# A fused long-convolution and gated-MLP kernel: first rows in four transfers, the norm's power by row tile on GpSimd, a new order of work, last waits in order of the stores

## The chip, the cores and the metric

One NeuronCore of a Trainium2 chip runs the whole program in one launch. The metric is device time in microseconds (us), from the start of an execution to its end. Engines are named as in the profile: PE (TensorE; PEld is its weight load), DVE (VectorE), ACT (ScalarE), POOL (GpSimd) and SP (SyncE, which here only issues DMAs; ACT issues some too).

## The reference

All tensors are bfloat16; x = A_q is 2048 x 512, the filter ssm_k is 512 x 2048, the MLP weights are 512 x 1792, 512 x 1792 and 1792 x 512.

```python
xn = (x - mean(x)) / sqrt(var(x) + 1e-5)             # over the 512 features
# A: H3 branch
k_shift[s] = sum over t<4 of k[s - 3 + t] * shift_k[:, 3 - t]
kv = k_shift * v
y = causal_convolution(kv, ssm_k)                    # by FFT of length 4096 over 2048 positions
s = xn * (y + kv * ssm_D)
# B: gated MLP on the same xn
g = silu((gelu_tanh(xn @ w_gate) * (xn @ w_up)) @ w_down)
out = x + s * g
```

## The kernel before, in words

**Layout.** Partition p holds rows 16p to 16p+15 of x, k, v and the output, so "row tile t" (t = 0 to 15) is row 16p+t of every partition. Row tiles are worked in four groups q of four.

**The norm, `ln(q)`, line 805.** For each row tile `bn_stats` (L808) and `bn_aggr` (L809) on DVE put mean and variance into `mv`. For q = 0 the four tiles go in two halves of two, for q > 0 all four at once: DVE adds the epsilon (L816), POOL raises to the power -0.5 (L817), and DVE normalises each tile (`XN`, L820). For q = 0 and 1 PE transposes each XN tile (L841) into `xnT`; for q = 2 and 3 a DMA transpose does.

**The filter and the convolution.** The filter arrives in four pieces h0 to h3 of 128 channels (`Hn`). PE transposes them (L865), ACT or DVE copies the result to `HTr`, and PE multiplies it by the first stage F1 of a two-stage transform (`stage1`, line 900). The results go to DRAM scratch `ZH` by DMAs that ACT issues and come back rearranged as `BH` for the second stage. The product kv takes the same road: `kshift(i)`, line 939, makes k_shift * v for the four row tiles of group i on DVE (a product into `KAC`, L956; three products into `KTM`, L960, each added to KAC, L962; the product with `V`, L964). It needs the loads k0 to k(i), v(i) and the taps. `stage1("K", u)` multiplies V by F1 on PE, ACT or DVE copies it to `AST` or `ASX`, and SP stores it to `ZK` (line 923). `spectrum(n)`, line 1028, multiplies the two spectra and goes back through `ZI`.

**The MLP.** `unit(q, m)`, line 1060: four matmuls with Wg and four with Wu, ACT's gelu (L1088) and DVE's product `HT` (L1091). `down(q)`, line 1094: 14 matmuls with Wd a row tile, then ACT and DVE (`G`, L1115 and L1117; L1123, L1125 and L1126 for the last group).

**What sets the order.** All work is declared as tasks. `SEQ` is a string of task numbers that was written by a search over the cost model in `Sched`; `Sched.run` (line 344) walks it, gives each task its engine and buffers, and the tasks are then emitted in that order. So the order in which an engine meets its instructions is the order of SEQ alone, and every engine works in order. In the model the input loads (`load`, line 580) have a queue of their own, called "loads". In the program that is emitted, they are DMAs issued by SP, in the same instruction stream as SP's stores and reads of scratch, and a wait of SP for a store's data holds up what stands behind it. SP's stream in the kernel before: x00 (row tiles 0 and 1), h0, x01 (tiles 2 and 3), h1, wg0, wu0, h3, wg1, x1, the first halo of k, wu1, h2, sk, second halo, wg3, k0, kz, wu3, wg2, wu2, D, k1, v0, k2, wd0, v1, k3, v3, v2, wd1; then the first ZK store (K0), which waits for ACT's copy to AST; then x3, the first BH, further stores, reads and transposes; at the end the 11 output stores and a wait for each. "wg1" is the second chunk of w_gate, of 512 columns.

**PE's start.** PE runs `N_WARM` matmuls on zeros (`warm_up`, line 660) before its first real work.

```python
        for t in order:
            t.emit(t.eng)
        for d in d_out:
            trk.wait_direct("SP", d.sem, d.count)
```

## Time and profile before

| what | value |
|---|---|
| median of 3 runs (lowest, highest) | 196.63 us (196.54, 197.39) |
| the profiled execution's own time | 196.41 us |
| its span, first to last instruction | 194.6 us |
| PE busy | 188.7 us (97%) |
| DVE busy | 156.7 us (81%) |
| ACT busy | 125.0 us (64%) |
| POOL busy | 11.9 us (6%) |
| DMA, mean over the span | 247 GB/s |

The span leaves 1.8 us of the profiled execution's time outside. Busy time counts instructions that compute, not waits or the issuing of DMAs. An engine's line in the profile gives start, duration, engine, line of the program, operation and tiles (out<-in).

### The profile page before, as it was taken

The numbers are of one execution on the slowest core, as the hardware profiler recorded it, in microseconds if no ns is written. First come the engines' busy times: TensorE is split into PE (matmuls) and PEld (weight loads), VectorE is DVE, ScalarE is ACT, GpSimd is POOL, SyncE is SP. The second block draws the span as 40 slices with busy tenths as digits, with TensorE's granted clock in tenths as the row PEclk, the third lists the DMA queues.
The fourth block names the chain that finished last, engine by engine and source line by source line (L and its number), as shares of the span: only waits on it lengthen the run. The fifth ranks groups of instructions, "written<-read, shape, count | busy, mean of one in ns | idle before, by whom it ended". The sixth has DMA issues, their size and how long they took to land.

```text
span 194.6 us, 3488 instructions
## 1 busy us (share of the span) xinstructions
PE 188.7 (97%) x1379; PEld 87.2 (45%) x1393; DVE 156.7 (81%) x242; ACT 125.0 (64%) x173; POOL 11.9 (6%) x26
## 2 busy tenths in 40 slices
PE   7999999999999999999999999999999999999993
PEld 2694645544444444443444343434343444444442
DVE  6898799999999997768897894788694850988984
ACT  4788897677679688876777756967674532303031
POOL 7310600000000000020200000000000000000000
PEclk9999999999999999999999999999999999999999
DMA  5999999997769967999999618986132616647363
GB/s 182 330 329 339 362 381 403 410 406 257 303 190 342 156 178 251 343 327 287 277 284 274 243 54 258 332 280 217 56 111 109 214 61 231 251 121 253 117 267 108
DMA packets 34502, 48.14 MB, mean 247 GB/s; under 512 B 8499, under 2 KB 27191, under 8 KB 34486
## 3 DMA queue, kind: packets, MB, share of 16 engines
q1 hardware_dynamic: 28982, 39.53, 63.6%
q10 hardware_dynamic: 5504, 8.39, 11.9%
q8 instruction: 11, 0.18, 0.4%
q14 instruction: 5, 0.04, 0.1%
HBM read 27.39 MB, written 14.68 MB: 216 GB/s over the span
## 4 chain that ended last, share of the span: by engine, by line
PE 93%; DVE 2%; DMA 2%; POOL 1%; issue 1%; ACT 0%
PE psall L604 86%; PE psall L979 5%; DMA X<-in_A_q_dram 2%; PE psall L865 1%; PE psall L841 1%; POOL mv L817 1%; DVE stats L808 1%; DVE G L1126 0%; DVE G L1125 0%; ACT G L1123 0%; DVE XN L820 0%; DVE mv L809 0%; DVE mv L816 0%
## 5 line engine op out<-in xcount | busy, mean ns | idle before, releaser
L604 PE MATMUL psall<-xnT,Wu 128*128 128x512 bf16 (+1 forms) x232 | 55.5, 372 | 0.0
L604 PE MATMUL psall<-xnT,Wg 128*128 128x512 bf16 (+1 forms) x232 | 55.3, 372 | 0.0
L604 PE MATMUL psall<-Wd,HT 128*128 128x512 bf16 (+2 forms) x228 | 51.0, 366 | 0.9 <-issue 0.6
L1091 DVE TENSOR_TENSOR HT<-psall,GE 128x512 bf16<-128x512 f32 x54 | 36.3, 686 | 13.1 <-PE psall L604 11.1
L1088 ACT ACTIVATE GE<-psall 128x512 bf16<-128x512 f32 x54 | 31.2, 599 | 16.5 <-PE psall L604 14.1
L604 PEld LDWEIGHTS psall<-Wd,HT 128*128 128x128 bf16 x238 | 22.1, 98 | 26.3 <-issue 1.9
L604 PEld LDWEIGHTS psall<-xnT,Wu 128*128 128x128 bf16 x232 | 21.8, 98 | 25.7 <-issue 1.8
L604 PEld LDWEIGHTS psall<-xnT,Wg 128*128 128x128 bf16 x232 | 22.1, 98 | 24.9 <-issue 1.1
L595 ACT ACTIVATE HS<-psall 128x1024 bf16<-128x1024 f32 x15 | 14.7, 1022 | 4.5 <-PE psall L979 4.5
L595 ACT ACTIVATE BO<-psall 128x1024 bf16<-128x1024 f32 x12 | 12.0, 1023 | 6.9 <-PE psall L979 6.9
L962 DVE TENSOR_TENSOR KAC<-KAC,KTM 128x2048 bf16<-128x2048 bf16 x12 | 14.6, 1219 | 0.1
L960 DVE TENSOR_TENSOR KTM<-KK,SKB 128x2048 bf16<-128x2048 bf16 x12 | 14.6, 1219 | 0.1
L595 ACT ACTIVATE KB<-psall 128x1024 bf16<-128x1024 f32 x11 | 10.9, 1023 | 5.5 <-PE psall L979 5.5
L1117 DVE SCALAR_TENSOR_TENSOR G<-G,psall 128x512 bf16<-128x512 bf16 x12 | 7.9, 683 | 6.7 <-ACT G L1115 6.7
L595 ACT ACTIVATE AST<-psall 128x1024 bf16<-128x1024 f32 x10 | 10.1, 1023 | 3.5 <-PE psall L604 3.5
L808 DVE BATCH_NORM_STATS2 stats<-X 128x6 f32<-128x512 bf16 x16 | 10.4, 681 | 0.8 <-DMA X<-in_A_q_dram 0.8
L1115 ACT ACTIVATE G<-psall 128x512 bf16<-128x512 f32 x12 | 7.0, 600 | 6.2 <-PE psall L604 6.1
L1042 DVE TENSOR_TENSOR HS<-KB,HS 128x1024 bf16<-128x1024 bf16 x16 | 10.9, 683 | 0.0
L1042 DVE TENSOR_TENSOR HW<-KB,HW 128x1024 bf16<-128x1024 bf16 x16 | 10.9, 687 | 0.0
L817 POOL TENSOR_TENSOR mv<-mv,NHALF 128x4 f32<-128x4 f32 (+1 forms) x5 | 5.7, 1148 | 83.0 <-DVE mv L816 83.0
L1123 ACT ACTIVATE G<-psall 128x512 bf16<-128x512 f32 (+2 forms) x5 | 2.6, 513 | 12.3 <-PE psall L604 12.3
L598 DVE CAST KB<-psall 128x1024 bf16<-128x1024 f32 x5 | 6.1, 1223 | 4.2 <-PE psall L979 4.2
(78 smaller groups left out, 179.3 us busy)
## 6 DMA issues: line engine op xcount, KB each, us to landing
BH<-ZH SPq DMA_DIRECT2D x8, 512.0 KB, 5.4
HW<-HS SPq DMA_DIRECT2D x16, 256.0 KB, 2.7
BK<-ZK SPq DMA_DIRECT2D x8, 512.0 KB, 5.9
ZI<-BO ACTq DMA_DIRECT2D x16, 256.0 KB, 2.6
BI<-ZI SPq DMA_DIRECT2D x8, 512.0 KB, 4.2
ZK<-AST SPq DMA_DIRECT2D x5, 512.0 KB, 3.4
Hn<-in_A_ssm_k_dram SPq DMA_DIRECT2D x4, 512.0 KB, 7.2
KK<-in_A_k_dram SPq DMA_DIRECT2D x4, 512.0 KB, 12.4
```

The lines of the kernel that those rows point to most:

```text
L595: return h.activation(o, i, ACTF.Copy, scale=scale)
L604: return h.matmul(o, lhsT=l, rhs=r, start=st, stop=sp)
L808: t_stats[t] = op([("DVE", 670.0)], lambda e, h, t=t: h.bn_stats(stats[:, t, :], X[:, t, :]), r=[bX[q][t % 4]], w=[bst[t]], rr=[R_X[t]], w ...
L817: t_pw = op([("POOL", 850.0)], lambda e, hd, ts=ts, n=n: hd.tensor_tensor(mv[:, ts, 3:4], mv[:, ts, 2:3], NHALF[:, 0:n, :], ALU.pow), r=[b ...
L960: op([("DVE", dur)], lambda e, h, j=j, m=m: h.tensor_tensor(KTM[:, m.slot, :, :], kk(j), sk(j), ALU.mult), r=need + [bSKB[j], a], w=[m], r ...
L962: op([("DVE", dur)], lambda e, h, m=m: h.tensor_tensor(KAC[:, a.slot, :, :], KAC[:, a.slot, :, :], KTM[:, m.slot, :, :], ALU.add), r=[m], ...
L979: trk.op("PE", lambda h: h.matmul(ps(s, i)[b, :], lhsT=wt(col)[a, :], rhs=data(col)[a, :], start=n < 16, stop=n >= len(todo) - 16, tile_po ...
L1042: return hd.tensor_tensor(o, flat(KB, kb[h]), o, ALU.mult)
L1088: op([("ACT", act(512))], lambda e, h: h.activation(GE[:, g.slot, :], bank(pg), ACTF.Gelu_apprx_tanh), r=[pg], w=[g], rr=lambda: R_bank(pg ...
L1091: op([("DVE", dve(512, 1))], lambda e, h: h.tensor_tensor(HT[:, q % 2, m, :], bank(pu), GE[:, g.slot, :], ALU.mult), r=[pu, g], w=[bHT[q][m]],
L1115: op([("ACT", act(n))], lambda e, h, g=g, pc=pc: h.activation(g, pc(), ACTF.Tanh, scale=0.5), r=[p], w=[bt], rr=lambda p=p: R_bank(p), ww= ...
L1117: op([("DVE", dve(512, 1))], lambda e, h, g=g, pc=pc: h.scalar_tensor_tensor(out=g, in0=g, scalar=1.0, in1=pc(), op0=ALU.add, op1=ALU.mult ...
```

## The change

- The first four row tiles are loaded in four transfers of 128 KB in place of two of 256 KB (`load_x0`). SP's stream becomes x00, x01, h0, x02, x03, wg0, wu0, h1, x1, wg1, first halo, h3, wu1, second halo, h2, sk, k0, kz, wg3, wu3, D, k1, wg2, wu2, k2, v0, wd1, wd0, v3, v1, then K0 (the first ZK store), then v2 and k3, then the first BH, x2 and so on.
- In the norm the epsilon and the power are two POOL instructions; for q = 0 they and the buffers are by row tile, and for q > 0 for four at once. DVE's addition is gone.
- The warm-up has 9 matmuls in place of 11. They read 128 columns of zeros four times over, so that the first memset is of 128 columns and the rest of it follows.
- The two products that build a table (`m_prod`, before at L701) are declared behind the four XN tiles of q = 0 (line `S.behind(t, ...)`).
- The model's landing times of the first five loads are given as numbers (`LANDS`), and SEQ is a new string: the order changes on every engine, throughout.
- The last waits of SP stand in the order in which the stores were issued.

```diff
-N_WARM = 11
-ORDER = "x00 x01 w0 w1 h0 h1 h2 h3 D0 w2 ..."
+N_WARM = 9
+ORDER = "x00 x01 h0 x02 x03 h1 w0 w1 h2 h3 D0 w2 ..."
 SEQ = (
...
+    LANDS = (3000.0, 3450.0, 5100.0, 5550.0, 6250.0)
...
+                if n_loads < len(self.LANDS):
+                    free[eng] = self.LANDS[n_loads] - self.LOAD_LAT
+                n_loads += 1
...
-        t_zero = S.add([("DVE", 250.0)], lambda e: trk.op("DVE", lambda h: h.memset(ZERO, 0.0), w=[R_zero]), w=[bwarm])
+        S.add([("DVE", 130.0)], lambda e: trk.op("DVE", lambda h: h.memset(ZERO[:, 0:128], 0.0), w=[R_zw]), w=[bzw])
+        S.add([("DVE", 200.0)], lambda e: trk.op("DVE", lambda h: h.memset(ZERO[:, 128:512], 0.0), w=[R_zero]), r=[bzw], w=[bwarm])
...
         def load_x0(t, ring):
-            load(f"x0_{t}", X[:, 2 * t:2 * t + 2, :], x_dr[:, 2 * t:2 * t + 2, :], R_X[2 * t:2 * t + 2], bX[0][2 * t:2 * t + 2], 262144, ring)
+            load(f"x0_{t}", X[:, t, :], x_dr[:, t, :], [R_X[t]], [bX[0][t]], 131072, ring)
...
-            for h in range(1 if q else 2):
-                n = 4 if q else 2
-                ts = slice(4 * q + 2 * h, 4 * q + 2 * h + n)
+            for h in range(1 if q else 4):
+                n = 1 if q == 0 else 4
+                ts = slice(4 * q + h, 4 * q + h + n)
...
-                t_var = op([("DVE", 180.0)], ... hd.tensor_scalar(mv[:, ts, 2:3], mv[:, ts, 1:2], LN_EPS, None, ALU.add) ...)
-                t_pw = op([("POOL", 850.0)], ... hd.tensor_tensor(mv[:, ts, 3:4], mv[:, ts, 2:3], NHALF[:, 0:n, :], ALU.pow) ...)
+                def pw(e, ts=ts, n=n, rm=rm):
+                    trk.op(e, lambda h: h.tensor_scalar(mv[:, ts, 2:3], mv[:, ts, 1:2], LN_EPS, None, ALU.add), r=rm, w=rm)
+                    trk.op(e, lambda h: h.tensor_tensor(mv[:, ts, 3:4], mv[:, ts, 2:3], NHALF[:, 0:n, :], ALU.pow), r=rm + [R_nh], w=rm)
+                S.add([("POOL", 430.0 + 230.0 * n)], pw, r=[bid, *bm], w=[b])
...
-        t_ln = ln(0)
+        ln(0)
         S.add([("ACT", 2400.0)], m_turn, r=[bMF], w=[bMF2])
+        for t in tm_tasks:
+            S.behind(t, [d for b in bXN[0:4] for d in b.writers])
...
-        for d in d_out:
+        for d in sorted(d_out, key=lambda d: trk.ev_order[d.sem.name, d.count]):
             trk.wait_direct("SP", d.sem, d.count)
```

## The prediction

> **What bounds the kernel now.** I read the page first, then the chain that ended last, then the waits of PE, then the timeline at three places.

> ```profile
> PE 188.7 (97%) x1379; PEld 87.2 (45%) x1393; DVE 156.7 (81%) x242; ACT 125.0 (64%) x173; POOL 11.9 (6%) x26
> ...
> PEclk9999999999999999999999999999999999999999
> ...
> PE 93%; DVE 2%; DMA 2%; POOL 1%; issue 1%; ACT 0%
> ```

> PE is the bound: 93% of the chain is PE following itself, at full granted clock. The waits of PE between 8 and 190 us add up to 0.6 us. So the time can only move in three ways: real work starts earlier, PE gets a hole that it doesn't have now, or the tail behind PE changes. The chain begins and ends so (start, length, what):

> ```profile
> 0.72 3.02 DMA X<-in_A_q_dram
> ...
> 3.77 1.29 DVE stats L808 x2
> ...
> 5.56 1.64 POOL mv L817
> ...
> 7.22 0.42 DVE XN L820
> ...
> 7.69 0.72 PE psall L841 x8
> ...
> 183.28 7.42 PE psall L604 x37
> ```

> The timeline of the start shows the warm-up, the table's product beside the first power, and a later power (start, length, engine):

> ```profile
> 5.38 1.22 DVE L701 TENSOR_TENSOR TM<-TAB 128x1024 f32<-128x1024 f32 x1
> 5.56 1.63 POOL L817 TENSOR_TENSOR mv<-mv,NHALF 128x2 f32<-128x2 f32 x1 [0.79 <-DVE mv L816]
> ...
> 5.84 1.39 PE L865 MATMUL psall<-ident,Hn 128*128 128x128 f32 x8
> ...
> 9.66 0.70 POOL L817 TENSOR_TENSOR mv<-mv,NHALF 128x2 f32<-128x2 f32 x1 [2.47 <-DVE mv L816]
> ```

> The same power takes 1.63 us beside a DVE product and 0.70 us later. The third place is where SP meets its first wait, at the store K0 (SP's queue, then DVE, then the DMAs issued between 54 and 56.5 us with their time to landing):

> ```profile
> 54.25 0.33 SPq L576 DMA_DIRECT2D ZK<-AST  x1
> 54.62 0.43 SPq L576 DMA_DIRECT2D X<-in_A_q_dram  x1
> 55.18 0.71 SPq L576 DMA_DIRECT2D BH<-ZH  x1
> ```
> ```profile
> 58.51 1.22 DVE L956 TENSOR_TENSOR KAC<-KK,SKB 128x2048 bf16<-128x2048 bf16 x1
> ```
> ```profile
> SPq L576 <- ACT AST L595: 26.8, 3, 21.2
> ```
> ```profile
> ZK<-AST SPq DMA_DIRECT2D x1, 512.0 KB, 3.0
> X<-in_A_q_dram SPq DMA_DIRECT2D x1, 512.0 KB, 5.2
> BH<-ZH SPq DMA_DIRECT2D x1, 512.0 KB, 6.0
> ```

> The reader is to see that SP stands still for 21.2 us before K0, that now no input of kshift stands behind K0, and that the third of three transfers of 512 KB there lands 6.95 us after K0's issue (55.18 + 6.0 - 54.25). In the kernel before, DVE begins group 3 (the product with k3) at 58.51 without a wait; k3 had been issued at 26.9.

> **The change, part by part.** All sums are against the profiled execution, 196.41 us (span 194.6 and 1.8 around it), 0.22 below the median shown.

> *v2 and k3 behind K0.* This is the step that decides. In the new SP stream K0 stands ahead of v2 and k3, so these two loads, issued from 26.9 to 32.5 us before, now wait for ACT's copy to AST. K0 needs the second pair of V matmuls of unit 0. Behind the last of these: 0.38 us until it is done (379 ns is the mean of a 512-column matmul), 0 to 0.6 for the gelu that stands ahead of the copy in ACT's order (I take 0.6), and 1.05 from the copy's start to K0's issue (53.20 to 54.25): K0 is issued 2.0 us after that V matmul. In the new PE order 44 more matmuls of 512 columns follow it (45 x 0.216 = 9.7 us), then a Wg group that needs the PSUM bank that DVE's G product frees. So PE arrives 7.7 us after K0's issue. In DVE's new order that G product stands third behind k3's landing: KAC 1.14 (58.51 to the next at 59.65), KTM 1.13, G 0.68 and some 0.05, 3.0 us in all. And k3 is the third transfer behind the wait, as BH was: K0 plus 6.95. PE's hole is 6.95 + 3.0 - 7.7 = 2.25 us, and as PE has no slack anywhere it goes to the end.
> Bounds: if the second and third transfer follow K0's 3.0 us at the distance at which BH followed X (1.4 us), k3 lands at K0 plus 5.8 and the hole is 1.1. If k3 takes the 8.5 us of the K1 store issued at 59.64, the slowest of its neighbours, behind the 0.93 us of two issues, the hole is 4.7. I take 2.25: BH is the same place in the same queue. The low end is unlikely, since in the new order ACT issues one more 512 KB ZH store right beside K0. DVE itself stands still for nearly 4 us there; its later work is covered as long as PE's hole covers it.

> *The front.* DVE's first tile statistics can't begin before C's phase is done (3.72 us), one tile is 0.69 instead of 1.29, the aggregate 0.2, the epsilon on POOL between 0.10 (a memset) and 0.54 (a 128x128 tensor_scalar; I take 0.3), the power at most 0.70, as the table's products now stand behind the XN tiles. XN of tile 0 begins at some 5.8 instead of 7.22: 1.4 us of gain on offer. Also 2 warm-up matmuls of 0.43 go, and h0, second behind 256 KB as before, lands at 5.1 to 5.7. But the load queue takes the gain back. Up to the first matmul on wu1 PE has 24 filter transposes of 0.110, 16 others of 0.056, 42 matmuls of 0.109 and 14 of 0.216 before, 11.14 us, and PE is there at 18.20; wu1 landed at 18.07 (8.13 + 9.93). After, two matmuls of 0.109 more stand in front, and the same 4,432 KB are loaded up to and with wu1, so it lands at the same time: the gain is at most 0.3 us. And h3 moves from the seventh load (2,560 KB, 11.56 us) to the twelfth (3,920 KB). The queue had brought 3,584 KB at 15.63 and 3,920 KB at 16.86; PE reaches h3 at about 15.7 with 9.4 us of work done, and if h3 lands at 16.86 the front loses 0.5. I take 0 between a gain of 0.3 and a loss of 0.5. Two more issues (0.46 us each on SP) shift the first loads behind them, which are 4 to 12 us in the queue anyway.

> *Epsilon and power on POOL, q > 0; the table.* DVE loses 5 additions of 0.17. POOL gets 7 more instructions, 0.1 to 0.5 each, at 6% busy. For q = 1 the XN tiles come up to 0.5 later than 20.1 to 24, and PE's transposes of them are at 28.5 and later; q = 2 and 3 have tens of us. The table TF, done at 14.6, would be 4 us later and is read first by ACT at 60. Nothing on the path; if the q = 1 cover were gone it would cost at most 0.5.

> *The last waits.* The last store is issued at 192.41 and lands 1.54 later. SP's long wait (1.03 us) ends at 193.98, and three further waits and a branch, all long met, end at 194.24. In the new order the last store's wait is last: 0.27 less one wait of 0.03 to 0.06. I take -0.2; between 0 and -0.27.

> *Sum:* 196.41 + 2.25 + 0 - 0.2 = 198.5 us. Everywhere else both orders are made of the same matmuls with 48 changes between full and tiled matmuls, so PE's own work is the same.

> **The rivals.** *k3 in time, no change.* If k3 lands by K0 plus 4.7, DVE's G product is done before PE asks for it and the hole is nil: 196.41 - 0.2 + 0 = 196.2, from 195.9 to 196.7 with the front's bounds; not slower. For it: in the slice of 53.5 to 58.4 us the DMAs moved 190 GB/s, far from the 410 they can, and K0 alone took 3.0 us. Against: the X load right behind K0 took 5.2, and BH 6.0.
> *The front pays and k3 is in time: faster.* If wu1 and h3 land earlier than the byte count says, the 1.4 us come through: 196.41 - 1.4 - 0.2 = 194.8. For it: x1 and the halo came slowly before (848 KB from 13.08 to 16.86, where 512 KB take 1.3 to 1.5 elsewhere). Against: the DMA row is full from 5 to 43 us, so what one load saves the next one needs.
> *The clock.* At first PE runs at half rate: 11 warm-up matmuls in 4.88 us, 0.43 each against 0.216, and the first eight filter transposes 1.39 us against 0.89 in the chain for the next eight. With 9 warm-ups and about 1 us of idle PE before XN, full clock may come later, or be lost in the hole. A late clock makes up to 2 us of early work cost twice; the wait for h3 hides some 1 us of that: 198.5 + 1 = 199.5. Lost behind the hole for as long as the slow start lasted, from 1.17 to about 6.5 us, half of 5.4 comes on top: 198.5 + 2.7 = 201.2. [...]

> **How the numbers follow.** Forecast 0.72, k3 in time 0.15, front pays 0.06, clock 0.07. The forecast's own range is 1.1 to 4.7 of hole, -0.3 to 0.5 of front, -0.2: 197.0 to 201.4; its upper fifth needs the slowest neighbour. For 8 in 10 I take 196.6 to 200.2: below lie most of "front pays" and part of "k3 in time", above the far end of the hole. Half a percent, 1.0 us, is what a measurement of this kernel can tell. Of the forecast's 0.72, 0.65 lies over 197.6. Slower 0.65 + 0.07 = 0.72; same 0.07 + 0.15 = 0.22; faster 0.06.

> **What would show it.** In the profile after: k3's issue within 1 us behind the first ZK store, at 52 to 54 us; DVE idle for 3 to 5 us with the k load as its releaser, in front of the KAC product; a PE hole of 1 to 4 us around 60 to 64 us that ends with DVE's G; XN of tile 0 at about 6 us; a wait of PE for h3 or wu1 between 15 and 19 us; 0.2 us less behind the last landing. The prediction is wrong if DVE meets k3 without a wait, or if PE has other work than I counted while DVE stands still.

## The result, and the profile after

The changed kernel takes 199.97 us (median of 7 executions, 198.34 to 201.8); the kernel before, beside it, 196.63 (196.39 to 197.39). The ratio is 1.0145, with a 95% interval of 1.0119 to 1.0172; the medians of all seven give 1.017. The seven fall in two groups. Three have a granted clock of 1.0 and take 198.34 to 199.06; four have 0.991 and take 199.97 to 201.8. The profiled execution is one of the second group: 201.2 us, span 199.4. A comparison leaves out executions that it takes for disturbed, here the one of 201.8 and in a later set all those at 0.991, so the executions of both groups are given throughout.

First the waits of PE between 8 and 196 us (in all, times, longest) in the kernel before and in the changed one, then DVE's between 40 and 80 us in the changed one:

```profile
PE psall L604 <- issue: 0.6, 4, 0.2
```
```profile
PE psall L609 <- DVE G L1125: 2.4, 1, 2.4
PE psall L609 <- issue: 0.6, 4, 0.2
PE psall L609 <- DVE HT L1099: 0.2, 1, 0.2
```
```profile
DVE KAC L964 <- DMA KK<-in_A_k_dram: 4.3, 1, 4.3
```

Where there was nothing over 0.6 us in all, one wait of 2.4 has come, and behind it stands DVE, which waits for the load of k. The chain of waits shows the same piece from the store to PE (start, length, what):

```profile
53.48 0.33 SPq L581
...
53.85 0.46 SPq L581
...
54.35 6.79 DMA KK<-in_A_k_dram
...
61.16 1.23 DVE KAC L964
62.39 1.14 DVE KTM L968
63.52 0.61 DVE G L1125
...
64.18 7.36 PE psall L609 x26
```

The store ZK is issued at 53.48, v2 at 53.85 and k3 at 54.35; k3 lands at 61.14, DVE does three products, and PE goes on at 64.18. What comes behind the hole is seen in PE's weight loads (start, length, engine), one for each matmul:

```profile
60.97 0.31 PEld L609 LDWEIGHTS psall<-Wd,HT 128*128 128x128 bf16 x2
64.17 0.13 PEld L609 LDWEIGHTS psall<-xnT,Wg 128*128 128x128 bf16 x2 [2.89 <-DVE G L1125]
64.58 0.15 PEld L609 LDWEIGHTS psall<-xnT,Wg 128*128 128x128 bf16 x1 [0.27 <-issue]
65.01 0.15 PEld L609 LDWEIGHTS psall<-xnT,Wg 128*128 128x128 bf16 x1 [0.28 <-issue]
...
67.14 0.15 PEld L609 LDWEIGHTS psall<-V,F 128*128 128x128 bf16 x1 [0.28 <-issue]
67.50 0.10 PEld L609 LDWEIGHTS psall<-V,F 128*128 128x128 bf16 x1 [0.20 <-issue]
67.71 0.53 PEld L609 LDWEIGHTS psall<-Wd,HT 128*128 128x128 bf16 x3
```

From 64.17 to 67.14 the loads follow each other at 0.43 us, from 67.50 on at 0.21: PE runs at half rate for some 3.3 us. The page's row of the clock has the dip at the same place (it has none for the half rate of the start: the trace's record of the clock begins with the first change, here at 9.38 us, and what lies ahead of that reads as full):

```profile
PEclk9999999999999799999999999999999999999999
```

The span is 4.8 us longer than before, and it divides by the starts of the weight loads. From load 300 to load 340 of the real work PE needs 12.79 us (58.81 to 71.60) where it needs 8.63 without a hole (57.73 to 66.36, in the kernel with 11 warm-ups below): 4.16. Of these 2.77 are the hole (2.99 between two loads in place of 0.22) and 1.39 the slow matmuls behind it. The rest of PE's delay is the start: the last load is at 196.13, less 4.16 that is 191.97, and in the kernel before it was at 191.19, so 0.78 (load 300 itself is 0.85 later than in the kernel before, where it is at 57.96). Behind DVE's last instruction the span goes on for 2.07 us instead of 2.22: -0.15. The sum is 2.77 + 1.39 + 0.78 - 0.15 = 4.79.

### The profile page after: what moved, and what is told of

It is laid out like the page before. It is cut to its first block, busy times and chain, and to the rows that moved or that the text cites. A ratio compares the mean times of both kernels' runs of the same rounds, so it can differ in the third digit from the quotient of the medians.

```text
span 199.4 us, 3501 instructions
## 1 busy us (share of the span) xinstructions
PE 190.9 (96%) x1377; PEld 88.3 (44%) x1391; DVE 157.8 (79%) x239; ACT 124.8 (63%) x172; POOL 14.4 (7%) x35
## 4 chain that ended last, share of the span: by engine, by line
PE 84%; DVE 4%; DMA 3%; POOL 3%; issue 2%; ACT 1%; SPq 0%; ACTq 0%; POOLq 0%
PE psall L609 76%; PE psall L987 5%; DMA KK<-in_A_k_dram 3%; PE psall L871 2%; PE psall L847 1%; POOL mv L825 1%; POOL mv L824 1%; DVE XN L828 1%; DVE HT L1099 1%; DVE KAC L964 1%; ACT AST L600 1%; DVE KTM L968 1%; DVE TM L707 1%; POOL C L689 0%; SPq L581 0%
## 5 line engine op out<-in xcount | busy, mean ns | idle before, releaser
L609 PE MATMUL psall<-xnT,Wg 128*128 128x512 bf16 (+1 forms) x232 | 57.5, 380 | 2.4 <-DVE G L1125 2.4
L609 PE MATMUL psall<-xnT,Wu 128*128 128x512 bf16 (+1 forms) x232 | 56.1, 372 | 0.2 <-DVE HT L1099 0.2
L609 PEld LDWEIGHTS psall<-xnT,Wg 128*128 128x128 bf16 x232 | 22.3, 99 | 28.5 <-issue 3.2
L600 ACT ACTIVATE HS<-psall 128x1024 bf16<-128x1024 f32 x15 | 14.6, 1022 | 4.4 <-PE psall L987 4.4
L970 DVE TENSOR_TENSOR KAC<-KAC,KTM 128x2048 bf16<-128x2048 bf16 x12 | 14.6, 1216 | 0.1
L968 DVE TENSOR_TENSOR KTM<-KK,SKB 128x2048 bf16<-128x2048 bf16 x12 | 14.6, 1214 | 0.1
L600 ACT ACTIVATE BO<-psall 128x1024 bf16<-128x1024 f32 x11 | 10.9, 1022 | 5.5 <-PE psall L987 5.5
L603 DVE CAST BO<-psall 128x1024 bf16<-128x1024 f32 x5 | 6.1, 1225 | 5.8 <-PE psall L987 5.8
L600 ACT ACTIVATE XN<-psall 128x512 bf16<-128x512 f32 (+1 forms) x11 | 8.6, 792 | 2.1 <-PE psall L609 2.0
## 6 DMA issues: line engine op xcount, KB each, us to landing
BH<-ZH SPq DMA_DIRECT2D x8, 512.0 KB, 4.8
BK<-ZK SPq DMA_DIRECT2D x8, 512.0 KB, 5.0
BI<-ZI SPq DMA_DIRECT2D x8, 512.0 KB, 4.2
ZK<-AST SPq DMA_DIRECT2D x5, 512.0 KB, 3.0
Hn<-in_A_ssm_k_dram SPq DMA_DIRECT2D x4, 512.0 KB, 7.4
KK<-in_A_k_dram SPq DMA_DIRECT2D x4, 512.0 KB, 10.6
```

The lines of the kernel that those rows point to most:

```text
L600: return h.activation(o, i, ACTF.Copy, scale=scale)
L603: return h.tensor_copy(o, i)
L609: return h.matmul(o, lhsT=l, rhs=r, start=st, stop=sp)
L968: op([("DVE", dur)], lambda e, h, j=j, m=m: h.tensor_tensor(KTM[:, m.slot, :, :], kk(j), sk(j), ALU.mult), r=need + [bSKB[j], a], w=[m], r ...
L970: op([("DVE", dur)], lambda e, h, m=m: h.tensor_tensor(KAC[:, a.slot, :, :], KAC[:, a.slot, :, :], KTM[:, m.slot, :, :], ALU.add), r=[m], ...
```

## The experiments

Orders are given as the order of SP's queue, in which K0 is the first ZK store. Ratios are to the kernel before, measured beside each set. In all kernels that only move a load, the streams of PE, DVE, ACT and POOL are those of the kernel they come from.

### The loads ahead of the store again

```diff
 load v1
+load v2
+load k3
 store K0
-load v2
-load k3
 load BH
```

> The changed kernel with one step undone: on SP's queue the loads v2 and k3 stand ahead of the first ZK store again; every other queue and engine is as in the changed kernel. Theory (store ahead of loads): DVE meets k3 without a wait, PE has no wait over 0.5 us between 58 and 68 us, and the granted clock is at least 0.998 in every execution, so also in those that lose 1.7 us behind the hole. The changed kernel's executions at clock 1.0 took 198.3 to 199.1; less the hole of 2.40 that gives 196.0 to 196.9, median 196.5, no different from the kernel before. Rival 1 (the start: half-rate work to 9.5 us is what costs): 198 or more, the hole only hides another wait. Rival 2 (a new wait behind it, since DVE or the stores come next): 197.2 to 198, with a PE wait of 1 us or more somewhere after 60 us.

Measured: 195.85 us (195.41 to 197.19, 12 executions), beside 196.33 for the kernel before: ratio 0.9979, interval 0.9963 to 0.9995. No execution is under a clock of 0.998. The timeline at the same place has neither of the two waits:

```profile
56.37 1.22 DVE L964 TENSOR_TENSOR KAC<-KK,SKB 128x2048 bf16<-128x2048 bf16 x1
...
58.64 0.68 DVE L1125 SCALAR_TENSOR_TENSOR G<-G,psall 128x512 bf16<-128x512 bf16 x1
...
61.25 1.89 PE L609 MATMUL psall<-xnT,Wg 128*128 128x512 bf16 x8
```

The product with k3 begins without a wait, G is ready 2 us before PE asks, and the whole loss is gone, the clock's part too. Both rivals fall: the start alone does not make the kernel slower than before, and no other wait takes the hole's place.

### The step alone, in the kernel before

```diff
 load v1
-load k3
 load v3
-load v2
 load wd1
 store K0
+load v2
+load k3
 load x3
```

> The kernel before with this one step alone: on SP's queue v2 and k3 stand directly behind the first ZK store; everything else as before. Theory: k3 lands 6.8 to 7.7 us after that store's issue at some 54.2, that is at 61.0 to 61.9, DVE stands still for 2.5 to 3.4 us ahead of the KAC product that began at 58.51, and its HT product of 62.04 comes at 64.5 to 65.4. PE's groups of Wd,HT and Wg that follow at 63.6 and 64.4 then wait 0.5 to 2.5 us: 197.1 to 199.1, and more by up to 1.7 in executions where the granted clock falls. Rival (in the old order of PE and DVE there is slack for it): the same time as before, 196.4 to 196.9, with DVE's wait but none of PE.

Measured: 198.09 us (197.9 to 198.84, 6 executions), ratio 1.009, 1.0073 to 1.0107: 1.76 us longer, clock 0.999 or more. Two lines of the timeline:

```profile
62.95 1.22 DVE L956 TENSOR_TENSOR KAC<-KK,SKB 128x2048 bf16<-128x2048 bf16 x1 [3.69 <-DMA KK<-in_A_k_dram]
...
69.59 1.02 PE L604 MATMUL psall<-V,F 128*128 128x512 bf16 x4 [1.08 <-DVE V L964]
```

k3 lands 8.0 us after K0's issue (54.92), where I had written 6.8 to 7.7, and DVE stands for 3.69. But PE does not meet it at Wg and Wd, as I had written; in the old order it meets it later, at the V product, with 1.08 and 0.36 us. The step is slow by itself, in either order; how much of DVE's delay PE sees depends on which product it needs next.

### k3 ahead of v2

```diff
 store K0
-load v2
 load k3
+load v2
```

> The changed kernel with k3 directly behind the first ZK store and v2 after it (the two exchanged, nothing else). Theory (the hole is the place of k3 in the queue): k3 lands about 1.4 us earlier, the distance of the third transfer to the second, so PE's hole is 0.7 to 1.4 us instead of 2.40: 196.9 to 197.9 at full clock. If the clock falls only after a hole over some 2 us, it stays at 1.0 in every execution, and the executions are all within 1 us of each other. If the clock falls after a hole of 1 us as well, some executions show 0.991 and are 1.7 us longer. Rival (the three transfers share the DMA engines and land together whatever their order): hole 2 us or more, 198 to 201 as the changed kernel.

Measured: 197.28 us (196.38 to 198.43, 10 executions), ratio 1.0057, 1.0032 to 1.0083, clock 0.997 or more in all. The waits of PE in the profile (the first is the one for h0 at the start):

```profile
PE psall L871 <- DMA Hn<-in_A_ssm_k_dram: 0.8, 1, 0.8
PE psall L609 <- DVE G L1125: 0.7, 1, 0.7
```

One place earlier in the queue, k3 lands 6.0 us after K0 (52.30 + 5.6 - 51.92) instead of 7.7 and the hole is 0.72: k3's place sets it. But the executions are of two groups, 196.4 to 196.8 and 197.8 to 198.4, which no theory had. To see the second, the kernel was profiled again:

> The changed kernel with k3 directly behind the first ZK store once more. Its first ten executions fell in two groups, 196.4 to 196.8 and 197.8 to 198.4, all at a clock of 0.997 or more, and the profile, of the fast group, had a hole of 0.72 us. If the groups are two places at which k3 lands, a profile of the slow one shows a hole of some 2.3 us in front of the Wg group; if they are two starts (the full matmul rate one step later), it shows half-rate matmuls up to 9.4 us or later and again a hole of some 0.7.

Measured: 197.44 us (196.68 to 198.7, 10 executions), ratio 1.0031, 1.0002 to 1.006, four of them over 198. The profile is again of the shorter group (196.84 us), with a hole of 0.7 and the full rate before 4.8 us. What the longer group loses stays open. It isn't the clock in the hole, since all 20 executions have 0.997 or more. A late full rate at the start remains possible, because the mean clock doesn't count it (the 0.991 of the changed kernel's profile is the 3.41 us at half rate behind the hole alone, not those up to 9.38); no profile shows the start of an execution of the longer group.

### 11 warm-ups, loads ahead

```diff
-N_WARM = 9
+N_WARM = 11
```

> The changed kernel with v2 and k3 ahead of the first ZK store and 11 warm-up matmuls instead of 9. Theory (the changed kernel's start is late because PE stands idle from 5.0 to 5.77 us and runs at half rate to 9.5 instead of 6.5): full rate is back by 6.5 to 7, the work up to the sixth F matmul is done at 8.3 to 8.7 us instead of 9.5, and the time is 0.4 to 1.0 us below the run with 9 warm-ups, 195.5 to 196.1. Rival 1 (the loads set the start, wu1 at 18.1): PE waits for wu1 or h3 between 15 and 19 us and the time is the same within 0.3. Rival 2 (the rate does not depend on the warm-ups): matmuls stay at half rate to 9.5 and the time is up to 0.3 longer.

Measured: 195.95 us (195.45 to 196.52, 12 executions), ratio 0.9977, 0.9967 to 0.9988. The work up to the sixth F matmul is done at 8.4, as the theory said, but the median is not below that with 9 warm-ups, as the first rival had it (without its waits for wu1 or h3); only the spread is less (1.1 us against 1.8). For the end of PE's slow start I read the profiles of all kernels together. Of the eight with 9 warm-ups, the full rate came before 5 us in three, at 5.95 in one and only at 9.3 to 10.4 in four. Of the six with 11, it came by 7.1 in all. Here are two with 9, the changed kernel and then the one with k3 first (start, length, engine):

```profile
5.77 1.09 PE L871 MATMUL psall<-ident,Hn 128*128 128x128 f32 x4 [0.77 <-POOL mv L824]
...
8.36 1.32 PE L609 MATMUL psall<-HTr,F 128*128 128x256 bf16 x6
```
```profile
5.54 0.69 PE L871 MATMUL psall<-ident,Hn 128*128 128x128 f32 x4 [0.84 <-DMA Hn<-in_A_ssm_k_dram]
...
7.34 0.83 PE L609 MATMUL psall<-HTr,F 128*128 128x256 bf16 x6
```

The same instructions, 1.32 against 0.83 us, because half rate lasted to 9.38 us in the one and ended before 5 us in the other. Load 60 of the real work is at 13.15 in the one and at 11.78 in the other.

### One more transfer ahead of k3

```diff
 load v2
-load k3
 load BH
+load k3
```

> The changed kernel with one more transfer ahead of k3: ZK store, v2, BH load, k3, all of 512 KB. Theory (the hole is k3's place in the queue, and the clock falls because PE stands idle): BH's landing in the changed kernel was 9.2 us after the store's issue, k3's 7.7; so the hole grows by up to 1.5, to 3.4 to 4.0 us, and now the clock falls in every execution: clock 0.99 or a little below throughout, 200.6 to 202.5 with no execution under 200. Rival (the clock falls by chance, not by the length of the hole): again about half of the executions at 1.0, these at 199.4 to 200.3. [...]

Measured: 202.52 us (201.42 to 203.39, 4 executions), ratio 1.0301, 1.0268 to 1.0333. The clock is 0.991 in the profiled execution and 0.983 in the other three, so by the mean those ran about twice as long at half rate. The windows around the hole (PE busy, then PEld, DVE, ACT, POOL, clock, DMA share, GB/s):

```profile
60.00:64.20 4.20, 0.68 (x4) 0.10 (x1) 2.92 (x4) 1.77 (x2) 0.00 (x0) 1.00 0.81 293
64.20:68.00 3.80, 3.71 (x11) 1.46 (x12) 3.80 (x6) 0.63 (x2) 0.00 (x0) 0.63 1.13 274
68.00:72.00 4.00, 4.00 (x18) 1.73 (x17) 3.93 (x4) 2.99 (x4) 0.00 (x0) 0.93 0.78 55
```

The wait is 3.62 us, and every execution loses the clock. In the profile PE's first loads behind the hole, from 64.3 to 65.2, still come at 0.22 us, and those behind them at 0.43: the rate falls about a microsecond after PE has begun again. The time, 202.52 us, is at the upper end of what I had written.

### The changed kernel again, and the hole filled

> The changed kernel itself, on the same chip as the three kernels beside it. From its first runs: about half of the executions at clock 1.0 and 198.3 to 199.1, the others at 0.991 and 200.0 to 201.8, with nothing between 199.2 and 199.9; PE's hole in front of the Wg group 2 to 3 us. If the clock does not depend on the hole (a limit on power, another chip's habit), the share of executions at 0.991 may be anything, but then the kernel with the hole filled shows it too.

Measured: two executions at clock 1.0 with 198.44 and 198.81 us, three at 0.991 with 201.46 to 202.19; hole 2.6. The ratio of 1.0105 (1.0088 to 1.0123) to the kernel before is that of the two at 1.0 alone.

```diff
-for m in range(m0, m1):
+for m in ([*range(m0, m1 - 1), *[m0] * 8, m1 - 1]
+          if (q, jt, m0) == (0, 2, 9) else range(m0, m1)):
```

> The changed kernel with eight more matmuls of 512 columns (the first Wd,HT matmul of the piece again, 1.73 us) directly ahead of the Wg group that waits; the down projection's sum of that one tile is then not the reference's, nothing else differs. Theory (idle PE is what costs the clock): the fillers lie in the hole, the wait shrinks from 2.4 to some 0.7, the end of the hole stays where it is, and no execution loses the clock: all at 0.998 or more, 198.2 to 199.2, so the median is 0.5 to 1.5 us below the changed kernel's although there is more work. Rival (the clock falls by load or by chance): executions at 0.991 and 200 or more remain, in about the same share.

Measured: 199.67 us (198.44 to 201.04, 6 executions), on the chip on which the changed kernel's median was 201.46. Its median is lower with 1.73 us more of work, though the two ranges overlap; the wait is 0.63. The theory had no execution at 0.991 and 198.2 to 199.2; one of six still has 0.991 (201.04), and three at full clock took 199.44 to 200.15. So a second kernel fills the hole whole, with 13 in place of 8:

> The changed kernel with 13 more matmuls of 512 columns (2.81 us) ahead of the waiting Wg group, where eight left a wait of 0.63 us in the profile and one execution of six at clock 0.991. The down projection's sum of that tile is again not the reference's. Theory (idle PE in the hole costs the clock): the wait in front of Wg is under 0.3 us in the profile and no execution is under 0.996. The time goes by the start, which differed by up to 1.9 us between the profiled executions with 9 warm-ups: 198.3 to 200.2. Rival (the clock falls by chance or by load): executions at 0.991 remain.

Measured: 199.93 us (198.31 to 200.37, 6 executions), none under 0.998. The windows of the changed kernel and then of this one:

```profile
60.00:64.20 4.20, 1.80 (x10) 0.61 (x8) 3.04 (x4) 2.83 (x4) 0.00 (x0) 0.98 0.90 321
64.20:68.00 3.80, 3.80 (x11) 1.44 (x12) 3.80 (x5) 0.60 (x1) 0.00 (x0) 0.58 1.00 308
```
```profile
60.00:64.20 4.20, 4.20 (x21) 1.86 (x19) 2.96 (x4) 2.75 (x4) 0.00 (x0) 1.00 0.90 322
64.20:68.00 3.80, 3.80 (x19) 1.74 (x18) 3.80 (x5) 1.91 (x3) 0.00 (x0) 1.00 1.00 309
```

PE is as late as with the hole (Wg at 64.33), but at full rate behind it. In both filled kernels the executions at full clock lie in two places, 198.3 to 198.5 and 199.4 to 200.4. Both profiles are of the later place, and in them the full rate of the start came only at 10.1 and 9.3 us; that the start makes the two places is likely, but no profile of the earlier place was taken.

Together the kernels give a row by the length of the hole in their profiles: without one, 0 of 48 executions lose the clock (the loads ahead, in four runs); with one of 0.6 to 1.1 us, 1 of 32; with 2.4 to 2.6, 7 of 12; with 3.6, 4 of 4; filled with 13 matmuls, 0 of 6. So the idle PE costs the clock. One reservation: in the last set the kernel before showed 0.99 in 2 of 30 executions (198.9 us), and with the last waits alone 0.991 in 2 of 12. No hole of this kind is there, none of the four was profiled, and their cause is open. So the clock can also fall without the hole, but in 4 of 42 executions there and not in 7 of 12.

### wg1 ahead of x1

In the kernel with the loads ahead and 11 warm-ups:

```diff
+load wg1
 load x1
-load wg1
 load kh1
```

> The kernel with v2 and k3 ahead of the first ZK store and 11 warm-ups, and now wg1 loaded ahead of x1 (the two exchanged). In that kernel PE waited 0.28 us (and with 9 warm-ups 0.77) at the first matmul on wg1, which landed at 13.1 (14.1). Theory (the load queue caps what the earlier start gives, at wg1): wg1 lands 1.2 us earlier, that wait goes, and the time falls by 0.2 to 0.5, to 195.4 to 195.8. Rival (x1 is late in its place: the statistics of the second tile group begin later, and PE waits for them or for a DVE product that has moved): no gain, or up to 0.5 longer, 195.9 to 196.5, with a PE wait between 20 and 30 us.

Measured: 197.0 us (196.32 to 199.51, 12 executions), ratio 1.0027, 0.9999 to 1.0055, where the kernel that it comes from has 0.9977 and 0.9956. wg1 lands at 11.3 and its wait is gone, but the timeline has two others:

```profile
13.49 1.29 DVE L814 BATCH_NORM_STATS2 stats<-X 128x6 f32<-128x512 bf16 x2 [1.61 <-DMA X<-in_A_q_dram]
14.69 0.41 DVE L1089 TENSOR_TENSOR HT<-psall,GE 128x256 bf16<-128x256 f32 x1
...
15.15 0.82 PE L609 MATMUL psall<-HTr,F 128*128 128x512 bf16 x4 [0.95 <-DVE HT L1089]
```

The rival's mechanism holds, at 15 us instead of 20 to 30 and with a greater loss than its 0.5: x1 lands at 13.4, DVE waits 1.61 us for it with an HT product queued behind the statistics, and PE waits 0.95 for that product. The load order of the start has no slack at either place.

### The last waits alone

```diff
-for d in d_out:
+for d in sorted(d_out, key=lambda d: trk.ev_order[d.sem.name, d.count]):
```

> The kernel before with one part of the change alone: SP's last waits in the order in which the stores were issued. Theory: the three waits behind the long one (0.27 us) go, less one wait of 0.03 to 0.06; the span's end lies 0.1 to 0.25 us closer behind the last landing, and the time is 0.1 to 0.25 below the kernel before. Rival (the end of the program waits for something else, so the order of the waits is free): no difference, within 0.05.

Measured: 196.79 us, beside 196.78; ratio 1.0008, 0.9978 to 1.0038, which can't tell 0.1% from nothing. The trace can: from the end of DVE's last instruction to the end of the span it is 2.05 us here and 2.06 to 2.08 in the eleven other profiles with the sorted waits, against 2.22 and 2.23 in two without. The part does what it says, and is worth 0.15 us.

> The kernel with v2 and k3 ahead of the first ZK store and 11 warm-ups once more, beside the last waits alone: what is left between the two is the start. From its first runs 195.5 to 196.5, median 195.95, where the kernel before had 196.33. If the start gives nothing, it is equal to the last waits alone; by the profiles (PE's last weight load at 190.90 against 191.19 in the kernel before) it is 0.2 to 0.4 below that.

Measured: 196.18 us (195.45 to 196.56, 12 executions), ratio 0.9956, 0.9935 to 0.9977. A version that beats both kernels is thus the changed one with v2 and k3 ahead of the store and 11 warm-ups, by 0.1 to 0.3% in the first comparison and 0.2 to 0.7% in the second. It is 0.6 us below the last waits alone, and the two intervals just don't overlap. PE's last weight load is at 190.99 against 191.70 there, and behind the start neither has a wait of PE over 0.2 us, so this part is gained at the start. Its size is uncertain: that last load differs by 0.5 between two profiles with the old start (191.19 and 191.70).

## Why the prediction was right, and where it was wrong

**v2 and k3 behind K0: right, and the step that decides.** K0 was issued at 53.48 (said: 52 to 54), k3 0.87 behind it, DVE stood 4.35 us (3 to 5), G was done 2.98 us after the landing (3.0), and PE came to the wait 7.9 us after K0 (7.7). The term that was mis-sized is the landing: 7.66 instead of 6.95, within its bounds. That makes the wait 2.40 to 2.77, as one counts, against 2.25. Moving the two loads back takes everything away, and moving them in the old kernel alone costs 1.76 us.

**The clock: the step that failed.** I priced it at nothing and gave it 7 in 100, but no run shows that a hole of 2.25 us leaves the clock alone: the kernel before has no hole (PE's waits between 8 and 190 us add up to 0.6). A wait of 2.4 to 2.6 us lost the clock in 7 of 12 executions. In the profile PE was busy for 1.20 us of the 3.41 up to the fall, so idle for 2.21 (shown below). The price was wrong too, on the other side: 1.39 us behind the hole, not 2.7, since half rate lasted 3.3 us and not 5.4. That the rival's sum is the profiled execution's 201.2 is luck: a late start and a longer hole make up what the clock did not cost.

The forecast of 198.5 is what the executions at clock 1.0 took (198.3 to 199.1, five of 12); the median lies above it mainly by this term. That it still lies in the range up to 200.2 is in part luck: three of the first seven executions were over that, and the second set has a median of 201.46. The groups' medians lie 1.8 us apart in the first set and 2.9 in the second, more than 1.39. What the rest is isn't shown; both profiles of the longer group have the late start, and the other group has no profile.

**The front: failed in two places.** "1.4 us of gain on offer" was DVE's gain, not PE's. XN came at 5.60 (said: 5.8), but in the kernel before PE had spent that time on filter transposes and stood idle for 0.46 only (PE in the kernel before):

```profile
7.69 0.72 PE L841 MATMUL psall<-ident,XN 128*128 128x128 bf16 x8 [0.46 <-DVE XN L820]
```

And "2 warm-up matmuls go" was booked as free, with the late clock left to a rival at 1 us; in four of the eight profiles with 9 the full rate came some 3 to 4 us later than in the kernel before (at 9.3 to 10.4 against 6.53), and in the profiled execution the front lost 0.78, outside my bound of 0.5. By the median this loss is not shown: with the loads ahead, 9 and 11 warm-ups take 195.85 and 195.95. That the load queue takes gains back was right, but at wg1 (waits of 0.28 and 0.77 us, landing at 13.1 and 14.1), not at wu1 or h3: no profile shows a wait for those.

**The last waits and the rest.** -0.15 where I took -0.2. Epsilon and power on POOL took 0.23 and 0.58 at the front, and behind the start no wait of PE over 0.2 us ends with what hangs on them; that they cost nothing there was right.

**The rivals.** k3 in time: no, it is 4.35 us late. The front pays: a little, with the loads ahead; these kernels are 0.4 to 0.6 us below the kernel before, and 0.15 of that is the last waits'. The sum with the measured terms, 196.41 + 2.77 + 1.39 + 0.78 - 0.15, is 201.2, the profiled execution.

## What to carry to other kernels

SP's queue issued in order, so every load behind the waiting store was as late as what the store waited for: k3, issued at 26.9 us in the kernel before, was issued at 54.35 behind K0 at 53.48. So a transfer that waits for nothing belongs ahead of the first that does, also where it had been early by 30 us. A hole of PE must be priced with what it does to the clock behind it: here 2.77 us of hole became 4.16 of delay. And an earlier input is worth only as much as the engine that sets the end had been idle for it: here XN came 1.62 us earlier (7.22 to 5.60), and PE had been idle for 0.46 of that.

## What the runs showed of the hardware

```profile
60.58:63.99 3.41, 1.20 (x6) 0.35 (x4) 2.83 (x3) 2.28 (x3) 0.00 (x0) 1.00 0.91 321
64.00:67.41 3.41, 3.23 (x8) 1.20 (x9) 3.41 (x5) 0.60 (x1) 0.00 (x0) 0.50 1.02 327
```
```profile
4.39:7.81 3.42, 1.89 (x18) 1.46 (x16) 2.60 (x8) 2.44 (x4) 1.90 (x5) 1.00 0.97 313
```

- Why the same hole cost the clock in 7 of 12 executions and not in the other five is not shown: no profile of the changed kernel is of an execution that kept the clock, and no run set the edges of the steps. That it depends on where the edges fall in the hole is my estimate, from the 3.413 us between them and the busy times of the two steps above.
- At the start, with 9 warm-ups, idle times of 0.70 to 1.36 us (as the timeline gives them) in front of the first transposes went with full rate at 9.3 to 10.4, one of 0.45 with 5.95; where the full rate had come during the warm-ups, idle times of 0.84 to 1.60 did not end it.
- The landing of the third transfer of 512 KB behind a store was 6.95, 7.66 (7.9 in the second profile) and 8.0 us after the store's issue in three kernels, with the same bytes ahead of it.
